# Spectrum pieces multiplied in place, turned products read back by halves, and a new written-out order in a convolution-plus-attention kernel

## The chip, the cores and the metric

The kernel runs on one core of one Trainium2 chip. A core has four engines that matter here, each with its own instruction stream worked off in order: PE (matrix multiply, whose weight loads are shown apart as PEld), DVE (vector), ACT (scalar and activation functions) and POOL. SP is a fifth stream, which in this kernel only issues DMAs. The engines wait for each other by semaphores. The metric is the device time of one execution in microseconds (us). The kernel before takes 303.53 us, the median of 9 runs between 301.97 and 305.27 us.

## What is computed

Two branches over the same input of 2048 rows by 512 channels are mixed by a gate:

```python
g = _sigmoid((x * gate_w).sum(-1, keepdims=True))
a = _A_ref(x, ...)            # long convolution of every channel
b = _B_ref(x, ...)            # linear attention with 32 heads of 16
return g * a + (1 - g) * b
```

Branch `a` builds a kernel of 2048 taps for each channel, `K = einsum("dn,dnl,dn->dl", Cc, exp(dt*A*l), dB).real`, pads it and the input to 4096, multiplies their Fourier spectra and transforms back; then it adds `u * Dskip`. Branch `b` forms `q, k, v`, applies for each head the feature map `concat(softmax(q @ w_phi), softmax(-q @ w_phi))` to `q` and `k`, sums `kv` and `z` over all rows, and divides the numerator by the denominator before the output projection `wo`.

## The kernel before

**Stages.** The work runs through these stages, which overlap. The *front* loads input (`UD`) and parameters, builds trigonometric tables (`TB`, `TI`, `TJ`), the factored tables `Ctab` and `Dtab` of the taps, and transforms the input (first step `psA` L577 to `XAu`, second step `psB` L225 to `XU`), writing the input's spectrum to memory (`XUd`). The *key stage* takes the 16 row tiles through `pk` (PE L695), two exponentials `Ek` (ACT), a reduction `Zk` (DVE L707), the values `vp` (PE L727) to `vb`, a scaling `vr` (DVE L736) and the sum `kvp` (PE L744). It ends when DVE reads `kvp` (`zj`, L820) and `Mw` is formed. The *query stage* takes four blocks of 512 rows: four `pq` (PE L879), exponentials `Eq` (ACT), sums `zs` (PE), a short chain `den` between ACT and DVE, a row of factors `apm` that goes through memory (`apd`) and comes back spread over partitions (`aexp`), a product of each `Eq` piece with it (DVE L943), and for each of four row tiles eight `bps` matmuls (L955) and four `diagD` ones (L958), evicted to `bS`.

**Taps and convolution** run beside these. There are eight groups `h` of 64 channels. For each half group DVE forms `A` (L991, with a sum L1006 for the last four groups) and `R` from the tables `E` and `cs` (L998, L1000, L1001); PE sums their products in `kps` (L212); the result is evicted as `KD`, transformed (`psA` L1041 to `XA`, `psB` L1082 to `XK`). The spectrum comes in pieces of 1024 columns: a piece `U` of the input's spectrum is loaded, and DVE multiplies it by `XK` into a tile `t` (L1104). PE turns this back by a first step (`psz` L1118, evicted to `Zr`), which SP writes to memory (`Zd`) and reads back with rows and times exchanged (`ZT`, L1137). The second step (`psy` L1171 and L1177) starts from the attention result `bS` of the same rows and channels, so that one DVE operation with the gate (`o`, L1201) gives the output, which SP stores (L1209). The last 64 channels skip the way through memory: their products `tN` are turned back on chip by 256 small matmuls (L1150, `Z`) and `psy` L1191.

**Three sets of 128 channels and two of 64** pass through `transform`; each of the first three gives two `o` tiles, the 64-channel sets give one each, eight in all.

**Buffers.** Four-kilobyte tiles per partition: `U` has 2 buffers and `t` 2. `Eq` is one tile for a whole query block, 2 buffers. `ZT` is one 8-kilobyte tile for a set, 2 buffers, in memory that is opened only after the query stage (`fpool`); every `psy` therefore comes after the last `bps`.

**What sets the order.** `Plan` collects the work as about a thousand nodes with dependences and named buffers. The string `ORDER` is the order in which all nodes are issued, and so the order of each engine's stream and of SP's DMAs. `SIDES` says for each of 129 evictions from the matmul accumulators (PSUM) whether ACT (L558) or DVE (L556) does it: 28 of them are on DVE. `RINGS` picks PSUM buffers. ACT changes its function table 12 times (L75), since exponentials and sines are in different tables.

Of the kernel before, what the change touches and what calls it, by code (L numbers as in the profile page):

```python
# [10 lines left out]
ACT = mybir.ActivationFunctionType  # L11
ALU = mybir.AluOpType
F32 = mybir.dt.float32
BF16 = mybir.dt.bfloat16
# [77 lines left out]
class Plan:  # L92
# [3 lines left out]
    ORDER = ("05020K0b0001080L0e0q0n0k0h0s0r0c0i0f0g04060t0l070d0m0o0O0N0Z0P0Q0R0-0S0p0M0T0_100U0V0W03091116171218130Y1419150X1a1b1c"  # L96
             "0u2x1p1d1i1e1j1f1k0a2D2E1w2F2G2H2I2J2L2M2N2O1l1S2K0j1q1t1u1r1v1s1L2P2R2S2Q2T2V1x2X1Q1z1y1A1B2U1E1O1C2W1R2Y2Z1D2_311F2-"
             "303334351M1G1N371H1I1P1K1T1V1g1h1J1m0y3639383a3b3c3d3e1U3f3g3h1W3i1X1Y2y3j3k3l3m3n3o3p3q0z3r3t1Z1-1_3s20213u223v232728"
             "3x3w3y292A2a242b252c3z3A2B0B0C2f2g320v0w0x2h2i2d3R3B2e2z0D2j2o2l2k2p2q3C3P3Q2n2s2r2m2t0A3S0E0F260G3D3E3G3F0H0I0J453J3M"
             "3N3H3I3K2u1n3L3O1o2v2w2C444b3-46473T639741424e4c4f3U4q4r8R8S3V4d8T4g4h4i4j4m8U4n4t4k4u8V8W4o4s4x4l4v4w4y4p4B4F4C4G4I4J"  # L100
             "4D8X8Y4z4A4E4U4V4H4K4L3_4M4X8Z3X40984Y914W924N4Q4O4R4S8-4_4P938_90949550534Z3Y999a969c9e4T9b9d9B9f4-9m575a5851549g5e52"
             "5955565b5c9C5f9h3W5d5m5n5p5i9o9i9D5q5g5h5o5r5j5k9j5t9E9k5s5x9n5u9p5y9l5l5B5C5E9F435v5F5z9G9q9r9t5D9u9s5G5w5I5A5Q5J5R5M"
             "5N5T5U5H9H9I5S5K9v9w5X5Y5O5_9J5V5L5P5W605Z619N5-62649O9K9P9x9y6566489z9AaPaRaSaW6768696b6a6d6c6e6f9T9UaQaUa29L9M9Q9V9R"
             "6g6i9W9X9Yada3a46ka5ae9S6hafa6496mag4aa7ao3Z6l6jah6naTaX6V6o9Z6XaV6W6p9-aY6Z6q9_6r6s6Y6taZb2b3b46ub5b96v6w6x6ybhbi6B6C"
             "a-a_6_b0b16D70bjb6a06-71b7b8babkblbb72bm6z6A6F7374bc6Ear756G6J6K7677a8as78a9bdbebfbgbn6Lboapai6Haqcvcwat6Ia16MajbCakbp"
             "bD6NcxcBbq6O6Pbtbubvcy6Q79cCaabz7a7bbAab7eac7fbrbKal7c7d7i6R7jam7kbscz7g7han7m7nbB7obLbM6Tbwau6ScEbxbEbyav6U7ycDbVaw7z"
             "bNbO7lbPbWaxbX7AaybF7CcAbG7B7E7p7qbYc47F7D7GcFc57sbZcMcN7Hb-7I7J7K7LbHbIbJcGdjc6cH7r7t7ubQc77v7wbR7M7NcScIcObScPcQc8c9"
             "7O7x8b8d7PcJ7Q7RbT8f7T8c8hcTcKcVcU7SducR7X8e8gcW8i8jcL8kcX8lb_8m7UbU7Vdkdl7Y7W8n7_7ZcYcZc08oc-c_d0ef7-8p8q8r80c1caegcb"
             "81828sc2dvc3dmdxdydnd18wd2dw8t8ucc83do8x8veld3d585d4d68AdpdI8y8B8CdqdJcd8z8EdFdrds8FdG8GdzdQ8DehdRdS8486dHdt878HemdKce"
             "dAdBdC88898ad7dT8I8KdDd8dUd9dE8J8LdddVen8M8Oewexde8Neyei8P8QejdadfdbdcdgekeHdhdLdMdWdXazeIeJaCdNcfaAcgdYaBaFaDeoepf1aE"  # L110
             "f2f3f4eqaGerescheteuf5evdZf7f8ezaKeKcleAaLeLf9faeBeMf6fbcmd-dOciaHdPd_eCeNeDaMaNficnfofccocpeOePeQeEeRe2fdaIeFaJfefgfh"
             "ffdie0flfmfjeGfkfne1aOe3e4cjfpfrfsckcqeSeTeUcreVcsctcufqe5ftfufvfwfxe6eaebe7e8eWeXeYe9fyecedeeeZe-fzfAfBfCe_f0")
    SIDES = ("0000010000011010100001110000010000001111110000000001000011001000000010000000000100011000000001000010000000000100010000"
             "00000010000")
    RINGS = ("1010110001110101000000000000000000100022222222222222222222222222222222000002222222222222222222222222222222200000000000"
             "0000000000000000000000000000000000000000000000000000000000000000003333333330030000003")
# [690 lines left out]
def queries_and_convolution(P, tc, nc, g, psum, sh, sp, sl, kv, bank, evict):  # L807
# [38 lines left out]
    mw = []  # L846
# [21 lines left out]
    for b in range(4):  # L868
        Q = Bag()
        eq = []  # L870
        for m in range(4):
            box = Bag()

            def pq(b=b, m=m, box=box, Q=Q):
                if m == 0:
                    Q.e = g.eqp.tile([128, 4, 2, 512], BF16, name="Eq", tag="r8")
                box.ps = bank("pq")
                for kt in range(4):
                    nc.tensor.matmul(box.ps[:], lhsT=g.Wqp[:, kt, 128 * m:128 * m + 128], rhs=g.xT[b][:, kt, :],  # L879
                                     start=(kt == 0), stop=(kt == 3))  # L880

            def qe(m=m, box=box, Q=Q):
                for sg in range(2):
                    act(out=Q.e[:, m, sg, :], in_=box.ps[:], func=ACT.Exp, scale=(1.0 if sg == 0 else -1.0))
                box.ps = None
            a = P.add("PE", 1.0, pq, [sh, sp, sk] + ([a] if m else []), take=["bk"] + ([] if m else ["r8"]))
            eq.append(P.add("ACT", 1.22, qe, [a], drop=["psum"], tab="L"))

        def zz(Q=Q):
            Q.z = g.psA.tile([128, 4, 128], F32, name="zs", tag="acc", bufs=1)  # L890
            for m in range(4):
                e = Q.e[:, m, :, :]
                for i in range(4):
                    nc.tensor.matmul(Q.z[32 * i:32 * i + 32, 0:2, :], lhsT=at.SZ[:, m, :], rhs=e[:, :, 128 * i:128 * i + 128],
                                     start=(m == 0), stop=(m == 3), tile_position=(0, 32 * i), skip_group_check=True)
                for sg in range(2):
                    for i in range(4):
                        nc.tensor.matmul(Q.z[32 * i:32 * i + 32, 2 + sg, :], lhsT=at.SS[:, sg, m, :], rhs=e[:, sg, 128 * i:128 * i + 128],
                                         start=False, stop=(m == 3), tile_position=(0, 32 * i), skip_group_check=True)
# [35 lines left out]
        for m in range(4):  # L935
# [6 lines left out]
            def de(m=m, box=box, Q=Q):  # L942
                nc.vector.tensor_tensor(out=Q.e[:, m], in0=Q.e[:, m], in1=box.x[:], op=ALU.mult)  # L943
                box.x = None
            x = P.dma(0.6, 1.8, ax, [zw], take=["ax"], move=2.2)
            em.append(P.add("DVE", 0.69, de, [x, eq[m]] + em[-1:], drop=["ax"]))
        for i in range(4):
# [3 lines left out]
            def pbm(b=b, i=i, box=box, Q=Q):  # L951
                box.ps = bank("bps")
                for k in range(8):
                    m, sg = k // 2, k % 2
                    nc.tensor.matmul(box.ps[:], lhsT=Q.e[:, m, sg, 128 * i:128 * i + 128], rhs=g.Mw[:, 4 * sg + m, :], start=(k == 0), stop=False,  # L955
# [13 lines left out]
            pb = P.add("PE", 2.1, pbm, em + [pb] + mw, take=["bk"] + (["x4"] if i == 0 else []), drop=(["r8", "x4"] if i == 3 else []))  # L969
# [85 lines left out]
    def transform(XA, ready, Q, off, nd, far, last):  # L1055
# [11 lines left out]
        for r0 in range(0, 32, ns):  # L1067
# [3 lines left out]
            def ld(r0=r0, box=box):  # L1071
                box.U = g.cpool.tile([128, 2, no, ns, 64], BF16, name="U", tag="U", bufs=2)
# [22 lines left out]
            def tt(r0=r0, box=box, end=end):  # L1095
                if far:
                    o = box.t = g.cpool.tile([128, 2, no, ns, 64], BF16, name="t", tag="t", bufs=2)
                    o = o[:]
# [10 lines left out]
            tn.append(P.add("DVE", 1.22, tt, [x, u] + tn[-1:] + ([] if far else [sq]), take=(["t"] if far else []), drop=["XK", "U"]))  # L1109
# [20 lines left out]
            z = P.add("PE", 1.03, fi, [tn[-1]] + ([z] if r0 else []), take=[psq, "Zr"], drop=["t"])  # L1130
# [3 lines left out]
        def fr(th):  # L1134
            if th == 0:
                F.Z = g.fpool.tile([128, 4096], BF16, name="ZT", tag="ZT", bufs=2)[:, 0:32 * nd].rearrange("p (t d) -> p t d", d=nd)
            nc.sync.dma_start(out=F.Z[64 * th:64 * th + 64], in_=F.Zd[:, 2 * th:2 * th + 2].rearrange("t x r d -> (x r) t d"))  # L1137
        for th in range(2 if far else 0):
            rn.append(P.dma(0.6, 1.8, lambda th=th: fr(th), wn + [sq] + [n.issue for n in rn[-1:]], take=(["Z"] if th == 0 else []), move=3.4 * nd / 128 + 0.3))
# [22 lines left out]
        for j0 in range(0, 16, nj):  # L1162
            box = Bag()
            end = j0 + nj == 16

            def py(j0=j0, box=box, end=end):
                if far:
# [5 lines left out]
                    for jj in range(nj):  # L1173
                        th = (j0 + jj) // 8
                        rows = slice(64 * th, 64 * th + 64)
                        for c in range(4):
                            nc.tensor.matmul(box.ps[32 * c:32 * c + 32, jj, :], lhsT=fc.TJ[rows, 4 * (j0 + jj) + c, :],  # L1177
                                             rhs=F.Z[rows, 4 * (j0 - 8 * th + jj) + c, :], start=False, stop=True, tile_position=(64 * th, 32 * c),
                                             skip_group_check=True)
                else:  # L1180
# [13 lines left out]
                if end:  # L1194
                    F.Z = None

            def ou(j0=j0, box=box):
                gb = g.gT[:, j0:j0 + nj]
                box.o = g.fpool.tile([128, nj, nd], BF16, name="o", tag="o", bufs=3)
# [7 lines left out]
            def st(j0=j0, box=box):  # L1207
                for c in range(4):
                    nc.sync.dma_start(out=ov[c, :, j0:j0 + nj, :], in_=box.o[32 * c:32 * c + 32])  # L1209
                box.o = None  # L1210
            y = P.add("PE", 1.15 if nj == 8 else 1.82, py, (rn[:1 + (j0 + nj - 1) // 8] if far else zn) + qdone[j0:j0 + nj] + ([y] if j0 else []), take=[psq, "o"],
                      drop=(["Z"] if end and far else []))
            o = P.add("DVE", 1.22, ou, [y], drop=["psum"])
            P.dma(1.95, 1.6, st, [o], drop=["o"], move=1.5)
# [22 lines left out]
def full_kernel(tc, A_u, A_A_re, A_A_im, A_B_re, A_B_im, A_C_re, A_C_im, A_log_dt, A_Dskip,  # L1237
# [7 lines left out]
    with ExitStack() as ctx:  # L1245
# [103 lines left out]
        def shift_keys():  # L1349
# [4 lines left out]
            g.eqp = pool(ca, "eqp", 2)  # L1354

        def shift_queries():
# [5 lines left out]
        P = Plan({"XAu": 1, "Ek": 2, "Zk": 2, "vr": 2, "vb": 2, "acc": 1, "r8": 2, "nrm": 1, "ax": 2, "x4": 5, "o": 3, "E": 4, "cs": 4, "A": 3, "R": 3, "KD": 1, "XA": 2,  # L1362
                  "XK": 2, "Z": 2, "Zr": 2, "U": 2, "t": 2}, {"ps": 2, "p0": 2, "bk": 3, "pf": 2})
# [63 lines left out]
```

## Time and profile before

| what | value |
|---|---|
| median of 9 runs | 303.53 us |
| the profiled execution | 302.38 us, span 300.5 us |
| DVE busy | 249.9 us (83%) |
| ACT busy | 236.2 us (79%) |
| PE busy | 218.6 us (73%) |
| 128x1024 eviction, DVE / ACT | 1.22 us / 1.02 us |
| 128x512 eviction, DVE / ACT | 0.68 us / 0.60 us |
| DVE first reads `kvp` (end of the key stage) | 130.57 us |
| last product L943 starts | 233.35 us |
| last `R` product starts | 268.64 us |

The span goes from the first to the last instruction of the profiled execution; the 1.9 us around it belong to its own time. "Idle before" is time in which an engine stood still just before an instruction, with the engine whose result ended it.

### The profile page before, as it was taken

How to read it: one execution, taken by the hardware profiler on the slowest of the kernel's cores; microseconds unless marked ns; L12 is line 12 of the kernel's file. 1: busy time of each engine (PE TensorE's matmuls, PEld its weight loads, DVE VectorE, ACT ScalarE, POOL GpSimd, SP SyncE). 2: the span in 40 equal slices, each digit the busy share in tenths (PEclk: the TensorE clock that was granted, in tenths of full speed). 3: DMA queues.
4: the chain of work that ended last, by engine and by line, in shares of the span. 5: the costliest groups of instructions: out<-in, count | busy, mean ns of one | idle time of the engine just before them, and what ended most of it. 6: DMA issues, size and time to landing. Idle time of an engine off the chain costs nothing.

```text
span 300.5 us, 10434 instructions
## 1 busy us (share of the span) xinstructions
PE 218.6 (73%) x4641; PEld 134.5 (45%) x4672; DVE 249.9 (83%) x401; ACT 236.2 (79%) x313; POOL 4.9 (2%) x17
## 2 busy tenths in 40 slices
PE   0056585347986999958988579999879978686960
PEld 0055464243432755542655434565544535454750
DVE  7849998899999899989878979989997958993431
ACT  2978998999999999798969799958888597446110
POOL 4000000000000000010000000000000000000000
PEclk9998959657998999986999999999999997779695
DMA  8996768969940000040231255553545746876933
GB/s 136 166 157 136 114 101 175 267 179 329 367 142 3 4 2 2 5 143 0 76 107 55 83 144 168 171 116 117 168 130 149 260 124 140 194 177 180 176 83 64
DMA packets 71357, 39.88 MB, mean 133 GB/s; under 512 B 57104, under 2 KB 63376, under 8 KB 71312
## 3 DMA queue, kind: packets, MB, share of 16 engines
q1 hardware_dynamic: 70256, 38.96, 52.7%
q8 instruction: 36, 0.59, 0.8%
q10 hardware_dynamic: 1056, 0.26, 0.6%
q14 instruction: 9, 0.07, 0.1%
HBM read 24.53 MB, written 14.94 MB: 131 GB/s over the span
## 4 chain that ended last, share of the span: by engine, by line
PE 39%; ACT 24%; DVE 15%; SPq 9%; issue 6%; DMA 4%; DVEq 0%; ACTq 0%
PE bps L955 9%; PE kps L212 6%; ACT E L83 5%; ACT cs L83 3%; PE pq L879 3%; ACT Ek L83 3%; SPq L1297 3%; DVE A L991 3%; ACT XU L558 2%; SPq L292 2%; PE psz L1118 2%; PE psB L1082 2%; PE vp L727 2%; PE psz L1150 2%; PE pk L695 2%
## 5 line engine op out<-in xcount | busy, mean ns | idle before, releaser
L991 DVE TENSOR_TENSOR A<-Ctab,Dtab 128x2048 bf16<-128x2048 bf16 x32 | 38.4, 1217 | 1.8 <-PE kps L212 1.8
L83 ACT ACTIVATE E<-args 128x1024 bf16<-128x1024 f32 x32 | 31.2, 1046 | 2.8 <-PE args L773 2.8
L83 ACT ACTIVATE cs<-args 128x1024 bf16<-128x1024 f32 x32 | 30.3, 1034 | 1.2 <-PE args L791 1.2
L955 PE MATMUL bps<-Mw,Eq 128*128 128x512 bf16 x121 | 29.0, 380 | 1.0 <-issue 1.0
L212 PE MATMUL kps<-R,A 128*32 128x64 bf16 x1536 | 26.8, 225 | 3.8 <-DVE R L1001 2.8
L577 PE MATMUL psA<-W,UD 128*64 128x256 bf16 x128 | 13.8, 380 | 20.7 <-DMA UD<-in_A_u_dram 18.7
L212 PEld LDWEIGHTS <-A 128*32 128x32 bf16 x1536 | 24.7, 152 | 8.6 <-issue 6.5
L998 DVE TENSOR_TENSOR R<-E,cs 128x1024 bf16<-128x1024 bf16 x32 | 21.9, 685 | 4.6 <-ACT cs L83 2.8
L1001 DVE TENSOR_TENSOR R<-E,cs 128x1024 bf16<-128x1024 bf16 x32 | 22.0, 688 | 0.6
L577 PEld LDWEIGHTS <-UD 128*64 128x64 bf16 x128 | 12.0, 206 | 22.0 <-DMA wc<-in_B_w_phi_dram 18.6
L707 DVE TENSOR_REDUCE Zk<-Ek 128x64 f32<-128x1024 bf16 x16 | 19.1, 1212 | 0.4 <-ACT Ek L83 0.4
L1104 DVE TENSOR_TENSOR t<-U,XK 128x1024 bf16<-128x1024 bf16 x28 | 18.0, 686 | 1.1 <-ACT XK L558 1.0
L83 ACT ACTIVATE Ek<-pk 128x512 bf16<-128x512 f32 x32 | 16.8, 606 | 1.8 <-PE pk L695 1.8
L955 PEld LDWEIGHTS <-Eq 128*128 128x128 bf16 x128 | 11.5, 98 | 15.1 <-issue 3.0
L83 ACT ACTIVATE Eq<-pq 128x512 bf16<-128x512 f32 x32 | 16.7, 627 | 1.7 <-PE pq L879 1.7
L695 PE MATMUL pk<-Wkp,xT 128*128 128x512 bf16 x59 | 16.5, 410 | 1.4 <-DVE vb L556 0.8
L225 PE MATMUL psB<-XAu,TB 64*128 64x128 bf16 x256 | 11.3, 245 | 8.2 <-ACT XAu L558 4.0
L727 PE MATMUL vp<-Wv,xT 128*128 128x512 bf16 x58 | 16.4, 394 | 0.6 <-issue 0.3
L1082 PE MATMUL psB<-XA,TB 64*128 64x64 bf16 (+1 forms) x640 | 12.2, 185 | 6.3 <-issue 1.6
L558 ACT CAST XA<-psA 128x1024 bf16<-128x1024 f32 x15 | 15.1, 1030 | 1.9 <-PE psA L1041 1.8
L1118 PE MATMUL psz<-t,TI 128*128 128x512 bf16 x50 | 15.6, 415 | 1.2 <-ACT XA L558 0.3
L558 ACT CAST Zr<-psz 128x1024 bf16<-128x1024 f32 x12 | 12.2, 1015 | 5.2 <-PE psz L1118 5.0
(179 smaller groups left out, 462.4 us busy)
## 6 DMA issues: line engine op xcount, KB each, us to landing
U<-XUd SPq DMA_DIRECT2D x16, 512.0 KB
XUd<-XUd SPq DMA_DIRECT2D x8, 512.0 KB
aexp<-apd SPq DMA_DIRECT2D x16, 256.0 KB
Zd<-Zr SPq DMA_DIRECT2D x14, 256.0 KB
XUd<-XU SPq DMA_DIRECT2D x8, 384.0 KB
ZT<-Zd SPq DMA_DIRECT2D x6, 512.0 KB
UD<-in_A_u_dram SPq DMA_DIRECT2D x4, 512.0 KB
out_dram<-o SPq DMA_DIRECT2D x32, 64.0 KB
```

Source lines behind the costliest of these rows:

```text
L83: i = self.nc.scalar.activation(**kw)
L212: nc.tensor.matmul(kps[32 * dj:32 * dj + 32, g4, e, :], lhsT=A[q][:, o, :, :, d].rearrange("p a b -> p (a b)"), rhs=R[ri][:, d, :], start= ...
L558: nc.scalar.copy(out=o, in_=i)
L577: nc.tensor.matmul(box.ps[64 * e:64 * e + 64, i, :], lhsT=g.UD[:].rearrange("p t (e g) -> p g e t", e=2)[:, gw * h + 4 * g4 + i, e, :], rh ...
L695: nc.tensor.matmul(box.ps[:], lhsT=g.xT[st // 4][:, kt, ss], rhs=g.Wkp[:, kt, :], start=(kt == 0), stop=(kt == 3))
L707: nc.vector.tensor_reduce(out=K.Z[:, u, :, :], in_=K.E[:, u, :, :].rearrange("p g (h f) -> p g h f", f=16), axis=mybir.AxisListType.X, op= ...
L727: nc.tensor.matmul(box.ps[:], lhsT=g.xT[st // 4][:, kt, ss], rhs=g.Wv[:, kt, :], start=(kt == 0), stop=(kt == 3))
L955: nc.tensor.matmul(box.ps[:], lhsT=Q.e[:, m, sg, 128 * i:128 * i + 128], rhs=g.Mw[:, 4 * sg + m, :], start=(k == 0), stop=False, skip_grou ...
L991: nc.vector.tensor_tensor(out=c.A[q][:].rearrange("p o a b d -> p (o a) b d"), in0=Ct.to_broadcast([128, 8, 8, 32]), in1=Dt.to_broadcast([ ...
L998: nc.vector.tensor_tensor(out=c.R[o][:, :, 32:64], in0=E[:, :, 32:64], in1=x, op=ALU.mult)
L1001: nc.vector.tensor_tensor(out=c.R[o][:, :, 0:32], in0=E[:, :, 0:32], in1=x[:, :, ::-1], op=ALU.mult)
L1118: nc.tensor.matmul(box.ps[:, hb], lhsT=fc.TI[:, k].rearrange("p t h a -> p (t h a)"), rhs=rhs, start=(k == 0), stop=(k == 1))
```

## The change

It has four parts. (1) The product of a spectrum piece is written over `U` itself; `t` goes, `U` has 3 buffers, and a buffer of `U` comes free after `psz` has read it instead of after the product. (2) `Eq` becomes four tiles for each block, 8 buffers of a quarter of the size; all four are given back together as before. (3) The turned products are read back by halves of the rows: each set of 128 channels fills two tiles of half the size, each by two DMAs, so 14 reads replace 8. The first half of the first two sets uses the tile `ZA`, in memory that exists during the query stage, so their `psy` needs only the first two query blocks, and its output is written over the tile's own first part. All others use `ZB`, 3 buffers, after the query stage. (4) New strings: another order for all engines and SP, another choice of evictions (37 of 129 on DVE, 28 before) and of PSUM buffers.

```diff
-    ORDER = ("05020K0b0001080L0e0q0n0k...
+    ORDER = ("050K080b090L0P0e020001040a...
...
-                    Q.e = g.eqp.tile([128, 4, 2, 512], BF16, name="Eq", tag="r8")
+                    Q.e = [None] * 4
+                Q.e[m] = g.eqp.tile([128, 2, 512], BF16, name="Eq", tag="r8")
...
-                box.U = g.cpool.tile([128, 2, no, ns, 64], BF16, name="U", tag="U", bufs=2)
+                box.U = g.cpool.tile([128, 2, no, ns, 64], BF16, name="U", tag="U", bufs=3)
...
-                    o = box.t = g.cpool.tile([128, 2, no, ns, 64], BF16, name="t", tag="t", bufs=2)
-                    o = o[:]
+                    box.t = box.U
+                    o = box.t[:]
...
-            z = P.add("PE", 1.03, fi, [tn[-1]] + ([z] if r0 else []), take=[psq, "Zr"], drop=["t"])
+            z = P.add("PE", 1.03, fi, [tn[-1]] + ([z] if r0 else []), take=[psq, "Zr"], drop=["U"])
...
-        def fr(th):
-            if th == 0:
-                F.Z = g.fpool.tile([128, 4096], BF16, name="ZT", tag="ZT", bufs=2)[:, 0:32 * nd].rearrange("p (t d) -> p t d", d=nd)
-            nc.sync.dma_start(out=F.Z[64 * th:64 * th + 64], in_=F.Zd[:, 2 * th:2 * th + 2].rearrange("t x r d -> (x r) t d"))
...
+        early = [nd == 128 and Q < 2 and hf == 0 for hf in range(2)]
+        zk = ["ZA" if e else "ZB" for e in early]
+        F.Z = [None, None]
+
+        def fr(hf, u):
+            if u == 0:
+                F.Z[hf] = (g.cpool if early[hf] else g.fpool).tile([128, 2048], BF16, name=zk[hf], tag=zk[hf], bufs=(1 if early[hf] else 3))[:].rearrange("p (t d) -> p t d", d=nd)
+            i = F.Zd[16 * u:16 * u + 16, 2 * hf:2 * hf + 2] if nd == 128 else F.Zd[:, 2 * u:2 * u + 2]
+            nc.sync.dma_start(out=F.Z[hf][64 * u:64 * u + 64], in_=i.rearrange("t x r d -> (x r) t d"))
...
+            ok = far and early[j0 // 8]
...
+                    if ok:
+                        box.o = F.Z[j0 // 8][:, 0:8]
```

What the new order moves, read from the two instruction streams: SP loads all four parts of `UD` ahead of the small parameters, and turns `wTq` ahead and `wTk` behind the writes of `pz`. DVE takes two `XAu` evictions ahead of its first parameter products, and the masks, `Wphi` and `diagD` move from the front's start to its middle. POOL makes `tgc` ahead of the small `one`. The first `A` product moves ahead of the selector `selE`, the second ahead of the first `Zk`. On ACT the eight `cs` of the second table set run before `KVT` and `Mw` instead of around them, and two `E` come ahead of the first `Eq`. The last table set's first `cs` come after the last `bps` tile of the third query block instead of after the second of the fourth. One `psy` with its `o` and its four stores goes into the query stage; the second `ZA` one stays in the end part.

## The prediction

> **What bounds the kernel now.** I read the page first, its busy times and its slices, then busy time by stretches of 20 us, then the sum of waits, and last the time line of DVE and of the end. No operation is removed, so the question is where engines stand idle.
>
> ```profile
> PE 218.6 (73%) x4641; PEld 134.5 (45%) x4672; DVE 249.9 (83%) x401; ACT 236.2 (79%) x313; POOL 4.9 (2%) x17
> DVE  7849998899999899989878979989997958993431
> ACT  2978998999999999798969799958888597446110
> ```
>
> ```profile
> 0.00:20.00 20.00, 1.33 (x13) 1.36 (x15) 13.03 (x50) 12.28 (x12) 3.56 (x15) 1.00 1.10 153
> ...
> 100.00:120.00 20.00, 18.68 (x494) 10.85 (x493) 19.78 (x26) 19.39 (x34) 0.00 (x0) 1.00 0.01 3
> ...
> 180.00:200.00 20.00, 19.57 (x262) 10.34 (x265) 19.21 (x27) 17.87 (x24) 0.00 (x0) 1.00 0.59 171
> ...
> 280.00:300.50 20.50, 10.06 (x494) 8.55 (x490) 5.01 (x5) 2.02 (x2) 0.00 (x0) 0.75 0.50 95
> ```
>
> In each stretch the numbers are PE, PEld, DVE and ACT busy. From 20 to 240 us DVE works 9 parts in 10 or more, ACT hardly less, and in the key stage (100 to 120 us) both are full. Around 180 to 240 us PE is full too. DVE's idle time up to 260 us, summed over the stretches, is 29.6 us, 7.0 of them before 20 us. The end is a chain of latencies: DVE works 5.0 us of the last 20.5.
>
> ```profile
> DVE R L998 <- ACT cs L83: 2.8, 1, 2.8
> DVE Eq L943 <- DMA aexp<-apd: 2.8, 4, 1.3
> DVE den L916 <- ACT den L83: 1.2, 2, 0.7
> DVE t L1104 <- ACT XK L558: 1.0, 3, 0.4
> DVE pb L499 <- ACT trg L83: 0.9, 1, 0.9
> DVE den L909 <- ACT den L83: 0.8, 1, 0.8
> DVE pb L490 <- ACT trg L83: 0.7, 1, 0.7
> DVE vr L736 <- ACT vr L83: 0.7, 2, 0.4
> DVE Zk L707 <- ACT Ek L83: 0.4, 1, 0.4
> ```
>
> These are DVE's waits for ACT and for `aexp` before its last `R` (total, times, longest). They are short and spread, and they are what a new order could save.
>
> **Nine evictions go from ACT to DVE.** By kind, five net are 128x1024 and four 128x512. DVE rows: 1.22 and 0.68 us; ACT rows: 1.02 and 0.60.
>
> ```profile
> L556 DVE CAST vb<-vp 128x512 bf16<-128x512 f32 x7 | 4.6, 683 | 0.2 <-PE vp L727 0.2
> L556 DVE CAST XK<-psB 128x1024 bf16<-128x1024 f32 x5 | 6.1, 1222 | 1.1 <-PE psB L1082 1.1
> L558 ACT CAST XA<-psA 128x1024 bf16<-128x1024 f32 x15 | 15.1, 1030 | 1.9 <-PE psA L1041 1.8
> ```
>
> DVE gains 5 x 1.22 + 4 x 0.68 = 8.8 us of busy time. On the time line neighbouring instructions overlap by about 0.08 us (two products of 1.22 take 2.35), so by starts it is 5 x 1.14 + 4 x 0.60 = 8.1 us. ACT loses 5 x 1.02 + 4 x 0.60 = 7.5.
>
> I added up DVE's work by starts in both instruction orders to three marks. To `zj`, the end of the key stage: 113.4 before, 120.1 after, +6.7. To the last L943: 201.8 and 212.8, +11.0. To the last `R`: 231.2 and 237.1, +5.9. Behind it 10.4 and 12.7, because one eviction of `Z` and one more `o` stand there.
>
> *To `zj`, +4.0 us.* Of +6.7 some fits into idle time. From 20 to 131 us the waits of more than 0.1 us that DVE's time line names sum to 5.2 us. ACT, lighter, can shorten those it causes; PE's and the DMAs' stay. I take half, 2.6: +4.0. Ends: +1.5 (all absorbed) and +6.7 (none). The front's changed loads: `UD` ends PE's first wait at 18.67 us; the small loads that stood ahead of three quarters of it cost SP 1.62 and 0.52 us, so PE may start up to 2.1 us earlier, or not at all where the transfers themselves set it. But DVE now has two `XAu` first and no `Wphi`; its wait for `wc` (3.9 us, to 18.90) becomes one for `psA`, at 18.67 + 1.14 less what `UD` gains, 17.7 to 19.8 us. That is -1.2 to +0.9; I take 0. Parameters queued behind `UD` delay ACT's `dtc` (17.34 before) and so DVE's L407, which now has 2.3 us of `XAu` ahead of it. `wTk` behind `pz` is needed by `Wkp` only, which moves to the end of the front; `pk` waits for it if it is late: 0, up to +2.0 (the row of one `wTq` issue, 1.97). POOL's `one` waits for `tgc` (2.0 us), before `w1`; PE needs that only at 18 us: 0.
>
> *From `zj` to the last L943, +4.4 us.* Before, 103 us hold 88.4 us of DVE work; after, 92.7. The additional work is not waste: more of the end's work is ahead of this mark. I leave the idle time of about 15 us as it is, since ACT has as much more to do there: two `E` ahead of the first `Eq`, and the last table load. PE has one `psy` pass (0.63 + 1.04), one `psz` (0.9) and one half `kps` (1.1) more ahead of the last `bps`. Bounds: half the 9.4 us of waits named there vanish (-0.3), or 5 us more arise at the joints of the stages (+9.4). One such joint is certain: all eight `cs`, 7.6 us, now stand ahead of `KVT`.
>
> *From the last L943 to the last `R`, -6.4 us.* Before, 35.3 us for 29.4 of work, with a wait of 2.8 for `cs` and 1.3 for `kps`. After, 24.3 of work. The first `cs` of the last set come earlier and that 2.8 us wait goes; but the third and fourth `cs` stand behind the second `bps` tile of the last block (2.5 us each on the time line), so DVE, after two sums and four `R`, waits for them some 1.5 us. Later ones stand behind `KD` and two `XA`. I take 4.6 us idle for 5.9. Ends: none of the gain in idle and 3 us more (-2.1), or 4.1 saved (-9.2).
>
> *The end, +0.7 us.*
>
> ```profile
> 269.39 1.10 PE L212 MATMUL kps<-R,A 128*32 128x64 bf16 x60 [0.80 <-DVE R L1001]
> 271.65 1.05 PE L1041 MATMUL psA<-W,KD 128*128 128x256 bf16 x8 [1.16 <-ACT KD L558]
> 280.29 3.59 PE L1150 MATMUL psz<-TI,tN 128*32 128x64 bf16 x133 [0.26 <-DVE tN L1104]
> 281.61 16.28 SPq L1209 DMA_DIRECT2D out_dram<-o  x20
> 292.59 1.23 DVE L1203 TENSOR_TENSOR o<-psy,gT 128x1024 bf16<-128x1024 f32 x1 [1.93 <-PE psy L1191]
> ```
>
> Here is the chain after the last `R`: `kps`, `KD`, `psA`, `XA`, `psB`, `XK`, `tN`, L1150, `psy`, `o`, stores. Only one `ZA` pass has left this part, while two passes that stood ahead of the last `R` now stand in it: six `o` become seven. One pass costs PE 1.67 us. It sits between `kps` and `psA`, where PE stood still 1.16 us: +0.5. All four `tN` now come without an `o` between them, -1.4; another `psy` splits L1150, +1.7; `Z` on DVE behind two `o`, about 0. Sum +0.8, and I take +0.7, as SP's last twelve stores may follow closely anyway. Ends -1 and +2.5.
>
> **What I cost at nothing.** The product in place is the same 28 instructions of 0.69 us. A `U` buffer comes free only after `psz`, so the next load, and on SP whatever stands behind it (`aexp`, `apd`), waits longer. SP waited 25.1 us in all for the product before; the cover is the third buffer, and most loads are issued a whole piece ahead. Without it, see the second rival; below nothing it can't go, as no wait of DVE was for `U`. The four `Eq` tiles come free together, so only the taking is finer: 0, at best the 1.7 us that ACT's `Eq` waited for `pq`. Six more reads cost SP about 6 x 0.62 us of issue (the median of L1137), in stretches where it waits anyway; at most 3.7.
>
> The Trainium skill, "DMA: Bandwidth & Descriptors", section "Anatomy of one DMA", gives a fixed cost of about 2.0 us for each DMA, nearly all of it the receipt; six more in series would by that be an estimated 12 us, which would turn the sum into +14.7. That page's figure is for DMAs issued from POOL, and no row here has such a wait in series.
>
> A second rule speaks against the change: "Perfetto Trace Analysis", section "Optimizing Scalar/DVE Operations", advises giving work to ScalarE when DVE is saturated, and here nine evictions go the other way. Taken strictly, all of DVE's +5.9 us would show and the sum would be +6.6. The rows show 29.6 us of idle DVE, so I don't take it strictly.
>
> **Sum.** +4.0 + 4.4 - 6.4 + 0.7 = +2.7 us on the profiled 302.38, that is 305.1. This execution lies 1.15 us under the median of 303.53; carried over, 306.2 us.
>
> **Rivals.** (A) *Faster: the lighter ACT ends DVE's waits for it.* The waits for ACT in the list above are 8.5 us without `aexp`. If all go, where I counted 3.9 of them as gone (2.6 and 1.3), the sum is +2.7 - 4.6 = -1.9, and with the 2.8 for `aexp` -4.7: 298.8 to 301.6. It decides from 4.2 us more than I counted. For it: ACT is 7.5 us lighter, and DVE's idle time is in many small pieces. Against: by 130 us ACT was itself full only because DVE fed it, and it is no earlier than DVE's `zj` lets it be. (B) *Much slower: SP holds the query blocks.* A `U` load waiting for `psz` keeps the next `aexp` behind it. DVE's longest wait for `aexp` was 1.3 us; once for each of four blocks, with the 2.5 us of a `bps` tile behind it at two of them, adds 5 to 10: 311 to 316. Against: only one `U` load stands between two `aexp` pairs. (C) *Nothing to measure:* PE, full from 180 to 240 us, sets the last `bps`, and DVE's additional work lies beside it; only the end's +0.7 and some 0.5 remain, 303 to 305. Half a per cent, 1.5 us, is about what can be told here.
>
> **Chances and range.** My own case 0.38, (A) 0.31, (B) 0.15, (C) 0.16. So faster 0.31, same 0.16, slower 0.53. The ends of the four terms sum to -9.0 and +16.5, which will not come together; taking in (A) and the near half of (B) the range is 298 to 312. My own case alone is 305.1 to 309.
>
> **What the profile after would show.** DVE busy near 258.8 us and ACT near 228.7; `zj` near 134.5 us instead of 130.57; the last L943 near 241.8; the last `R` starting near 270.5; then some 32 us to the end. If `zj` is at 132 or earlier, (A) is at work. If DVE waits more than 6 us for `aexp`, or SP's waits at the `U` loads hold the queue while `apm` is ready, (B). My forecast would be wrong above all if the joint at `KVT` or the `cs` behind `bps` cost another time than I took from their places in the order.

## The result, and the profile after

The changed kernel takes 306.16 us, the median of 16 runs between 303.67 and 308.81; beside it the kernel before took 302.86 us (51 runs). The ratio is 1.0098, with a 95% interval of 1.0074 to 1.0123: 1% slower, some 3 us. The profiled execution took 304.69 us (span 302.8), 2.3 us more than the profiled one of before. Medians are over all runs, ratios over the fast runs of both kernels, so the two can differ in the third digit. In the changed kernel line numbers behind `ORDER` are one higher up to the end of the key stage, two higher from the query stage on (the query product L943 is now L945), and 7 to 13 higher from the read-back on.

First the page of the changed kernel: busy times, then DVE, ACT and PE's granted clock in 40 slices.

```profile
PE 219.8 (73%) x4640; PEld 135.3 (45%) x4672; DVE 257.0 (85%) x410; ACT 228.9 (76%) x304; POOL 4.9 (2%) x17
...
DVE  7669999998999999997999879999968697995540
ACT  2879997958899999999969679967765885965000
...
PEclk9997765555899999995999759999987999979985
```

DVE gained 7.1 us and ACT lost 7.3, about what nine evictions weigh. The hole is in the three slices from 220 to 242 us (the 30th to the 32nd), where DVE is at 6, 8, 6 tenths and was at 9, 7, 9. The busy times by stretches (PE, PEld, DVE, ACT, POOL, granted clock, DMA share, GB/s) show it too: before, from 220 to 240 us, DVE was busy 17.18 us and PE 18.29, at a clock of 1.00.

```profile
0.00:20.00 20.00, 2.56 (x24) 2.59 (x26) 12.90 (x46) 11.92 (x11) 3.51 (x15) 1.00 1.12 153
100.00:120.00 20.00, 19.09 (x560) 11.53 (x566) 19.79 (x28) 19.91 (x31) 0.00 (x0) 1.00 0.01 3
180.00:200.00 20.00, 19.74 (x320) 10.62 (x322) 18.88 (x26) 19.09 (x26) 0.00 (x0) 0.99 0.60 159
220.00:240.00 20.00, 15.52 (x242) 8.24 (x241) 14.97 (x22) 12.97 (x15) 0.00 (x0) 0.83 0.52 140
280.00:302.80 22.80, 10.30 (x528) 8.13 (x528) 7.94 (x8) 1.01 (x1) 0.00 (x0) 0.78 0.51 96
```

Up to the end of the last `R`, DVE works 4.8 us more than before (243.9 instead of 239.1) and stands idle 2.5 us less (27.8 instead of 30.3); that is the 2.3 us. Many of its waits changed names: those for `aexp` (2.8 us) are gone, that for `cs` went from 2.8 us to 0.5, and others came. From the list of waits (total, times, longest):

```profile
DVE XA L557 <- PE psA L1043: 4.3, 2, 2.2
DVE XAu L557 <- PE psA L578: 3.2, 2, 2.5
DVE TJ L381 <- ACT tj L83: 2.3, 1, 2.3
DVE den L918 <- ACT den L83: 2.1, 4, 0.7
...
DVE ZA L1214 <- DMA U<-XUd: 1.7, 1, 1.7
```

The last one is named after a DMA, but DVE's time line shows what it is: the early `o` stands ahead of two query products and waits for its `psy`, which PE runs from 223.41 to 224.4 us.

```profile
222.36 0.42 DVE L919 TENSOR_TENSOR den<-zs,den 128x256 f32<-128x256 f32 x1
224.52 1.23 DVE L1214 TENSOR_TENSOR ZA<-psy,gT 128x1024 bf16<-128x1024 f32 x1 [1.73 <-DMA U<-XUd]
225.66 1.28 DVE L945 TENSOR_TENSOR Eq<-Eq,aexp 128x1024 bf16<-128x1024 bf16 x2
227.85 1.23 DVE L557 CAST XK<-psB 128x1024 bf16<-128x1024 f32 x1 [0.91 <-PE psB L1084]
```

The end looks as before, with one `o` more ahead of the last stores; from the end of the last `R` to the end of the span it is 31.2 us in both.

```profile
271.26 1.51 PE L213 MATMUL kps<-R,A 128*32 128x64 bf16 x64
...
273.89 1.05 PE L1043 MATMUL psA<-W,KD 128*128 128x256 bf16 x8 [0.20 <-ACT KD L559]
...
291.70 8.59 SPq L1222 DMA_DIRECT2D out_dram<-o  x12
...
293.65 1.22 DVE L1216 TENSOR_TENSOR o<-psy,gT 128x1024 bf16<-128x1024 f32 x1 [1.90 <-PE psy L1203]
```

The predicted marks stand against the measured ones so (us; the middle columns are differences to before):

| step of the sum | predicted | measured | mark in the changed kernel |
|---|---|---|---|
| start to `zj` | +4.0 | +3.8 | 134.35 |
| `zj` to the last L943 | +4.4 | +6.8 | 243.9 (the second of a pair from 243.32) |
| last L943 to last `R` | -6.4 | -8.3 | 270.94 |
| the end | +0.7 | 0.0 | span 302.8 |
| sum | +2.7 | +2.3 | |

By these marks the total holds, and so does the first term; the two in the middle miss by 2.4 and 1.9 us in opposite directions. Whether the marks mean what the prediction says was the question for the chip.

### The profile page after: what moved, and what is told of

Read it like the earlier page. It is cut to its first block, busy times and chain, and to the rows that moved or that the text cites. A ratio compares the mean times of both kernels' runs of the same rounds, so it can differ in the third digit from the quotient of the medians.

```text
span 302.8 us, 10446 instructions
## 1 busy us (share of the span) xinstructions
PE 219.8 (73%) x4640; PEld 135.3 (45%) x4672; DVE 257.0 (85%) x410; ACT 228.9 (76%) x304; POOL 4.9 (2%) x17
## 4 chain that ended last, share of the span: by engine, by line
DVE 35%; PE 24%; ACT 19%; DMA 10%; issue 5%; SPq 4%; DVEq 0%; ACTq 0%
PE bps L957 6%; DVE A L993 5%; DVE Zk L708 4%; ACT cs L83 4%; PE kps L213 4%; DVE R L1000 4%; DMA UD<-in_A_u_dram 3%; DVE R L1003 3%; DVE U L1106 3%; DMA XUd<-XUd 2%; DMA aexp<-apd 2%; DVE vr L737 2%; PE psz L1120 2%; SPq L1310 2%; PE psz L1158 2%
## 5 line engine op out<-in xcount | busy, mean ns | idle before, releaser
L957 PE MATMUL bps<-Mw,Eq 128*128 128x512 bf16 x120 | 30.1, 392 | 1.2 <-issue 1.1
L226 PE MATMUL psB<-XAu,TB 64*128 64x128 bf16 x256 | 14.1, 288 | 8.4 <-ACT XU L559 3.9
L1106 DVE TENSOR_TENSOR U<-U,XK 128x1024 bf16<-128x1024 bf16 x28 | 18.0, 685 | 1.4 <-ACT XK L559 1.4
L1120 PE MATMUL psz<-U,TI 128*128 128x512 bf16 x51 | 16.8, 431 | 3.1 <-DVE U L1106 1.8
L559 ACT CAST XK<-psB 128x1024 bf16<-128x1024 f32 x13 | 13.4, 1040 | 4.6 <-PE psB L1084 4.6
L226 PEld LDWEIGHTS <-TB 64*128 64x128 bf16 x256 | 12.3, 131 | 10.3 <-issue 7.1
L559 ACT CAST XA<-psA 128x1024 bf16<-128x1024 f32 x13 | 13.4, 1036 | 3.7 <-PE psA L1043 3.7
```

The costliest lines, as they stand in the source:

```text
L226: nc.tensor.matmul(ps[:, e, sl, :], lhsT=fc.TB[rows, r, 1 - ri:3 - ri, :].rearrange("p a b -> p (a b)"), rhs=XA[rows, r, ri, :], start=(ri ...
L559: nc.scalar.copy(out=o, in_=i)
L957: nc.tensor.matmul(box.ps[:], lhsT=Q.e[m][:, sg, 128 * i:128 * i + 128], rhs=g.Mw[:, 4 * sg + m, :], start=(k == 0), stop=False, skip_grou ...
L1106: nc.vector.tensor_tensor(out=o[:, k], in0=box.U[:, k], in1=box.XK[:].rearrange("p s (o d) -> p o s d", o=no), op=ALU.mult)
L1120: nc.tensor.matmul(box.ps[:, hb], lhsT=fc.TI[:, k].rearrange("p t h a -> p (t h a)"), rhs=rhs, start=(k == 0), stop=(k == 1))
```

## Experiments

All ratios are to the kernel before, run beside each kernel on the same chip. The marks compared below come from single profiled executions: in five kernels whose work up to `zj` is the same, `zj` lies between 129.1 and 131.0 us, so a mark tells differences of 2 us and more, not less. Diffs are shortened; where a line names a string or a stream in words, it stands for the recorded strings.

### Taking the structure apart from the order

**The product in place and four `Eq` tiles, in the old order** (`parts12`). The kernel before with the edits below; four `U` loads also stand a few places later on SP, behind the `psz` whose buffer they need.

```diff
-                box.U = g.cpool.tile([128, 2, no, ns, 64], BF16, name="U", tag="U", bufs=2)
+                box.U = g.cpool.tile([128, 2, no, ns, 64], BF16, name="U", tag="U", bufs=3)
...
-                    o = box.t = g.cpool.tile([128, 2, no, ns, 64], BF16, name="t", tag="t", bufs=2)
-                    o = o[:]
+                    box.t = box.U
+                    o = box.t[:]
...
+                Q.e[m] = g.eqp.tile([128, 2, 512], BF16, name="Eq", tag="r8")
```

> The kernel before with only the product written over `U` (three buffers, free after `psz`) and the four `Eq` tiles; order and evictions as before, except that four `U` loads stand a few places later on SP, behind the `psz` whose buffer they need. My theory, that these parts cost nothing: ratio to the kernel before 0.998 to 1.003, and DVE waits for `aexp` about as before (2.8 us). Rival (B), SP holds the query blocks: 1.015 to 1.04, with DVE waiting more than 6 us for `aexp`.

Measured: 308.41 us, ratio 1.0215 (1.0162 to 1.0267). What the prediction had costed at nothing costs twice as much as the whole change. SP's queue shows where. Here are its issues from 232 to 255 us in this kernel (start, length of the group with its waits):

```profile
232.12 0.38 SPq L1074 DMA_DIRECT2D U<-XUd  x1
234.75 0.32 SPq L1129 DMA_DIRECT2D Zd<-Zr  x1
235.17 15.77 SPq L1074 DMA_DIRECT2D U<-XUd  x2
251.00 4.04 SPq L1138 DMA_DIRECT2D ZT<-Zd  x2
```

and in the kernel before:

```profile
236.41 3.38 SPq L1073 DMA_DIRECT2D U<-XUd  x2
244.74 2.40 SPq L1137 DMA_DIRECT2D ZT<-Zd  x2
```

The second of the two `U` loads waits for a buffer, which now comes free only after `psz`; the reads of `ZT` stand behind it and issue 6.3 us later. The first `psy` on PE waits for them, and the first two `o` on DVE wait for theirs:

```profile
257.79 1.04 PE L1178 MATMUL psy<-ZT,TJ 64*32 64x128 bf16 x32 [5.80 <-DMA ZT<-Zd]
...
258.88 1.23 DVE L1202 TENSOR_TENSOR o<-psy,gT 128x1024 bf16<-128x1024 f32 x1 [2.80 <-PE psy L1178]
...
267.12 1.23 DVE L1202 TENSOR_TENSOR o<-psy,gT 128x1024 bf16<-128x1024 f32 x1 [2.95 <-PE psy L1178]
```

Before, these two waited 0 and 0.59 us. The last `R` stands behind them on DVE and ends at 274.9 us instead of 269.3. This is rival (B)'s mechanism with another victim: DVE's waits for `aexp` rose only from 2.8 to 5.4 us, and the block's products came 1.8 us later.

**The same with four `U` buffers** (`inplace4`). This takes away what the load waits for, and the four loads stand at their old places on SP again:

```diff
-                box.U = g.cpool.tile([128, 2, no, ns, 64], BF16, name="U", tag="U", bufs=3)
+                box.U = g.cpool.tile([128, 2, no, ns, 64], BF16, name="U", tag="U", bufs=4)
```

> As the run of the first two parts in the old order, but `U` has four buffers (the memory of the two `U` and two `t` before), so no `U` load moves on SP. Theory formed from that run: its 6 us come from one `U` load that waits 15 us on SP for `psz` at 235 us and keeps the `ZT` reads behind it; with four buffers the ratio to the kernel before is 0.997 to 1.004 and the first `ZT` read issues near 244.7 us again. Rival: the product over its own input, or the `Eq` tiles, cost the time themselves: 1.015 to 1.025.

Measured: 302.06 us, ratio 0.997 (0.9929 to 1.0011). The 6 us are gone: they were the missing buffer, with the later places of the loads that it forces, and neither the product over its own input nor the `Eq` tiles. Four `U` buffers are the memory of the two `U` and two `t` before. The change takes one of the four away and has the tile `ZA`, which is just as large; no run has both in the query stage.

**Besides, the reads by halves** (`halves`). The changed kernel's code for the reads, but with no half early and four `ZB`:

```diff
-        early = [nd == 128 and Q < 2 and hf == 0 for hf in range(2)]
+        early = [False, False]
```

> The run with four `U` buffers and, besides, the reads by halves of the rows (14 reads, `ZB` with 4 buffers, none of them early), each set's reads at the places of the old ones. My prediction, that six more reads cost nothing: 0.995 to 1.004. Rival: they cost SP's issue time in series, up to 3.7 us, or the receipt of each: 1.006 to 1.015.

Measured: 301.51 us, ratio 0.9965 (0.9932 to 0.9998). Six more reads cost nothing that can be told here; by the two intervals, a cost of some 1.5 us could hide. The Trainium skill, "DMA: Bandwidth & Descriptors", section "Anatomy of one DMA", has about 2.0 us of fixed cost for each DMA issued from POOL. The estimate of 12 us made from it does not show here: the reads, issued from SP, do not wait for each other in series (two of them issue within 1.34 us, from 254.57). With `inplace4`, from which it cannot be told apart, this is the fastest version in this study, 1.3% under the changed kernel; against the kernel before, its interval just excludes no gain.

### Taking the order apart at `zj`

**New up to `zj`, old behind** (`newkeys`). The two orders have nearly the same work ahead of `zj`, so they can be joined there:

```diff
 # kernel before
-    ORDER, SIDES, RINGS up to zj: as before
+    ORDER, SIDES, RINGS up to zj: as in the changed kernel
```

> The kernel before (old buffers, 8 reads, old order behind `zj`), but everything up to `zj` in the new order and on the new engines. My sum: `zj` at about 134.4 us and a ratio of 1.010 to 1.013. Rival, the later `zj` is work brought forward: 0.997 to 1.003.

Measured: 302.85 us, ratio 1.0027 (0.9992 to 1.0062). `zj` is at 134.25 us, 3.7 late as in the changed kernel, and the time is that of before. The delay melts behind `zj`: 2.2 us when PE ends the last `mps` matmul for `Mw`, 1.2 at the first query product, -0.2 at the last `R`. The last two are less than a mark can tell, but the ratio says the same. Some 2.2 us of it are work brought forward: the gate's `gz`, `gT` and `zrow` (1.0) and one `XA` (1.14), besides three `cs` on ACT (2.9).

**Old up to `zj`, new behind** (`oldkeys`). The changed kernel with the opposite edit:

```diff
 # changed kernel
-    ORDER, SIDES, RINGS up to zj: as in the changed kernel
+    ORDER, SIDES, RINGS up to zj: as before
```

> The changed kernel, but everything up to `zj` in the order and on the engines of the kernel before; from there on as changed. My sum (the key stage costs about 4 us, the rest gives some back): `zj` back at about 130.6 us and 3.5 to 4 us off the changed kernel, ratio to before about 0.996. Rival, suggested by the first L945, which the changed kernel starts at 167.2 us (before: 167.9): the later `zj` is only work brought forward, and the loss arises in the query stage; then the ratio stays at 1.006 to 1.012.

Measured: 308.28 us, ratio 1.0211 (1.0164 to 1.0259). `zj` is back at 130.60 us, and the kernel is 1.1% slower than the changed one: neither theory had that. DVE's list of waits names the place:

```profile
DVE XA L557 <- PE psA L1043: 9.4, 2, 6.2
```

The new order behind `zj` puts KVT and `Mw` behind all eight `cs`. Where three of them, and the gate, are not yet done by `zj`, PE ends the last `mps` matmul for `Mw` 16.1 us after `zj` instead of 9.2 in the changed kernel. The early `zj` is worth nothing to this order.

### Engines of the evictions

**The engines of before up to `zj`** (`oldsidesK`) and **behind it** (`oldsidesQ`), with the changed kernel's order untouched (one `XA` eviction keeps its new engine in both). For instance, of the string `SIDES`:

```diff
-    SIDES = ("0011000010010011010001011000010000100111111100000011000001...
+    SIDES = ("0000010000011010100001110000010000001111110000000001000001...
```

> The changed kernel, its order untouched, but the evictions up to `zj` on the engines of the kernel before: net three of 128x1024 and two of 128x512 go from DVE back to ACT, 4.6 us of DVE's work by starts. My theory: six tenths of it show, `zj` 2.5 to 3 us earlier and the time 2 to 3 us down, ratio to before about 1.000. Rival (DVE is not what sets `zj`, or ACT is as full): `zj` within 0.7 us of 134.4 and the ratio still 1.007 to 1.012.

> The changed kernel, its order untouched, but the evictions behind `zj` (from the last tile of `Mw` on) on the engines of the kernel before: ten go back to ACT and seven to DVE, net one of 128x1024 and two of 128x512, 2.3 us of DVE's work by starts. My theory of the prediction (DVE's added work shows): ratio 0.999 to 1.005. Rival, by the run with the key stage's engines: each eviction is where its order needs it, and it gets slower: 1.015 to 1.03.

Measured: 311.02 us, ratio 1.0272 (1.0211 to 1.0334), and 311.20 us, ratio 1.0278 (1.0224 to 1.0332). In both DVE has less to do (252.8 and 254.4 us busy instead of 257.0), and both lose 1.7 to 1.8% against the changed kernel; for the first, neither expectation had that. In the first, ACT takes two `XAu` ahead of the small `dtc`, and DVE stands longest there:

```profile
DVE pt L408 <- ACT dtc L83: 4.7, 1, 4.7
...
20.79 0.69 DVE L408 SCALAR_TENSOR_TENSOR pt<-Are,dtc 128x512 f32<-128x512 bf16 x1 [4.65 <-ACT dtc L83]
```

But this wait is not the loss. In the changed kernel DVE does the two `XAu` in that time, waits 2.46 us for the first, and starts the same `pt` at 20.87 us:

```profile
18.60 2.36 DVE L557 CAST XAu<-psA 128x1024 bf16<-128x1024 f32 x2 [2.46 <-PE psA L578]
...
20.87 0.68 DVE L408 SCALAR_TENSOR_TENSOR pt<-Are,dtc 128x512 f32<-128x512 bf16 x1
```

DVE's steps fall behind those of the changed kernel only after it, in many small waits: by 1.4 us at 32.3 us, 3.6 at 54.1, 4.5 at 102.6 and 5.8 at `zj` (140.16). Which of the 15 moved evictions starts this is not shown. In the second, one place tells most of it. A DVE eviction of `Mw` stands ahead of work that is ready:

```profile
145.00 1.23 DVE L557 CAST Mw<-mps 128x1024 bf16<-128x1024 f32 x1 [7.40 <-PE mps L854]
```

The `R` products behind it start at 146.15 us instead of 140.73, and the first query product and the last `R` come 6.3 us later. So an eviction can cost several times its 1.2 us by what it stands ahead of. The Trainium skill, "Perfetto Trace Analysis", section "Optimizing Scalar/DVE Operations", says that giving some work to ScalarE may make sense when DVE is saturated. In the changed kernel DVE is 85% and ACT 76% busy, and both ways of doing so cost time here: the share of busy time alone did not decide.

### The price of work on DVE

To price DVE's time by itself, four `A` products of the kernel before are done twice, once in the key stage (`dveK`), once between the first and the last query product (`dveQ`):

```diff
-                nc.vector.tensor_tensor(out=c.A[q][:].rearrange("p o a b d -> p (o a) b d"), in0=Ct.to_broadcast([128, 8, 8, 32]),
+                for _ in range(2 if q == 1 and h < 2 else 1):
+                    nc.vector.tensor_tensor(out=c.A[q][:].rearrange("p o a b d -> p (o a) b d"), in0=Ct.to_broadcast([128, 8, 8, 32]),
```

> The kernel before with four of the `A` products of the key stage done twice (same result), 4.6 us of DVE's work by starts ahead of `zj`, nothing else. Prediction's reading (six tenths of what DVE gets there shows, and stays): `zj` 2.7 us later and a ratio of 1.008 to 1.011. Rival (a late `zj` is recovered behind it): `zj` 2.5 to 4.6 us later and a ratio of 1.000 to 1.004.

> The kernel before with four `A` products between the first and the last query product done twice (the second `A` of both halves of the groups h = 4 and 5, same result), 4.6 us of DVE's work by starts, nothing else. If DVE sets this stage as it sets the key stage: last `R` 3.5 to 4.6 us later, ratio 1.011 to 1.015; the changed kernel's 2.0 us of added DVE work between its first product and its last `R` would then nearly all show. Rival (C) of the prediction, PE sets the last `bps` and DVE's idle time takes it in: last `R` 0 to 1.5 us later, ratio 1.000 to 1.005.

Measured: 306.09 us, ratio 1.013 (1.0085 to 1.0176), `zj` at 135.60; and 304.09 us, ratio 1.009 (1.0058 to 1.0122), last `R` 2.8 us later, though `zj` came 1.1 us earlier. A repeated product added a little more than the 1.14 us by which the expectations had it. The first of the four in `dveK`, and the same place before:

```profile
87.72 2.47 DVE L992 TENSOR_TENSOR A<-Ctab,Dtab 128x2048 bf16<-128x2048 bf16 x2
...
87.53 1.22 DVE L991 TENSOR_TENSOR A<-Ctab,Dtab 128x2048 bf16<-128x2048 bf16 x1
```

That is 1.25 us for each, 5.0 us for four. In the key stage all of it shows at `zj` (5.0 us), and 1.3% of 302.24, 3.9 us, at the end: 0.8 us for each us (0.5 to 1.1 by the interval). In the query stage it is 0.9% of 302.13, 2.7 us: 0.55 for each (0.35 to 0.75), between the two cases that were written down. The two intervals overlap, so that the key stage is dearer is likely, not shown.

### The early `psy`

**Moved back a little** (`latepsy`): its pass goes behind the first `bps` tile of the third block, and its `o` behind the two products it stood ahead of. SP's order stays.

```diff
 # PE
-psA, psy (early), psA, psB, args, bps
+psA, psA, psB, args, bps, psy (early)
 # DVE
-o (early), L945, L945, XK, U product
+L945, L945, XK, U product, o (early)
```

> The changed kernel with the early `psy` behind the first `bps` tile of the third query block and its `o` behind the two L945 products and the `U` product that it stood ahead of. Theory: the 1.7 us that DVE waits for this `psy`, and PE's pass ahead of `bps`, come off the last L945: 1 to 2.5 us less than the changed kernel, ratio to before 1.001 to 1.006. Rival: the chain `KD`, `psA`, `XA`, `psB`, `XK` sets this stretch: 1.008 to 1.012.

Measured: 308.76 us, ratio 1.0213 (1.017 to 1.0256), slower than the changed kernel by 1.1%, which neither expectation had. The two products do come directly behind `den`, but the four stores of this `o` still stand on SP ahead of the next `aexp`, and now wait themselves:

```profile
SPq L1222 <- DVE ZA L1214: 7.5, 1, 7.5
```

DVE then waits 3.0 us for `aexp`, and 3.3 for the `psy`. So the run says that a moved step takes its stores along, and leaves open what the early `psy` costs where it stands.

**Not early at all** (`noearly`, `noearly3`): the structure of `halves`, but the changed kernel's order and engines; what used `ZA` follows behind the query stage. The two differ in `U` alone:

```diff
-                box.U = g.cpool.tile([128, 2, no, ns, 64], BF16, name="U", tag="U", bufs=4)
+                box.U = g.cpool.tile([128, 2, no, ns, 64], BF16, name="U", tag="U", bufs=3)
```

> The changed kernel's order and engines, but four `U` buffers and no `ZA`: the reads, `psy`, `o` and stores that used it stand behind the query stage instead, all in `ZB` (4 buffers). Theory: with the old order this structure is 0.35% under the kernel before, so the rest is the price of the new order; without the early `psy` the last L945 comes 1.5 to 2 us earlier, one `o` more stands in the end, ratio to before 1.000 to 1.007. Rival: the new order lives on the early `psy`, and the end gets longer by the pass, its `o` and its stores: 1.012 to 1.020.

> The same with three `U` buffers, as in the changed kernel, nothing else. Theory: the new order already issues each `U` load behind the `psz` that frees its buffer, so the third and the fourth buffer differ by less than 0.3% here, unlike the 1.9% in the old order. Rival: the hold on SP costs here too, 1% to 2% over the run with four.

Measured: 308.23 us, ratio 1.0205 (1.0156 to 1.0253), and 307.50 us, ratio 1.0179 (1.0135 to 1.0223). In the new order the fourth buffer brings nothing that can be measured. And without the early `psy` the new order is some 1% slower than with it.

## Why the prediction was right, and where it was not

The time was right, 306.2 against 306.16 us, and so were the sign and, within half a us, three of the four marks (`zj`, the last `R`, the end); the last L943 came 2.1 us later than forecast. That the total came out to within half a us is partly luck: the two middle terms miss in opposite directions, and the reasons fared worse than the marks. A reading at the start is also too round: DVE works "9 parts in 10 or more" in seven of the eleven stretches from 20 to 240 us, and 16.93 to 17.44 us of 20 in the other four.

- **To `zj`, +4.0.** The mark was right (+3.8), its place in the sum was not. `newkeys` has the same late `zj` and ends within 0.3% of before. The step that failed is "of +6.7 some fits into idle time ... I take half": about 2.2 of the 6.7 us are work brought forward, and the remaining 4.5, though DVE's time in this stage is dear (0.8 by `dveK`), are paid for elsewhere. One payment is in the trace: from 18 us to `zj` DVE stands 5.1 us idle in `newkeys` (116.25 less 111.17 busy) and 7.9 before (112.57 less 104.69), and PE ends the input's transform at 56.7 us instead of 61.8. The front, which the prediction took as 0, gained: all six kernels with the new front and its engines stand idle 5.1 to 5.4 us there, the seven with the old one 6.7 to 8.6. The 1.7 us that are left are less than a mark can tell.
- **`zj` to the last L943, +4.4, and on to the last `R`, -6.4.** Measured +6.8 and -8.3: together -1.5 against -2.0. The mark between them falls where work of one order stands ahead of it and of the other behind. The first query product starts at 167.2 us, where it started at 167.9 before, so up to there nothing is lost; from it to the end of the last `R` the stage is longer. Here it is before, in `newkeys` and in the changed kernel (length, then busy PE, PEld, DVE, ACT, POOL, granted clock, DMA share, GB/s):

```profile
167.86:269.33 101.47, 87.09 (x1506) 49.15 (x1520) 89.88 (x128) 78.41 (x101) 0.00 (x0) 0.95 0.56 155
169.08:269.09 100.01, 87.56 (x1520) 48.70 (x1520) 89.80 (x128) 77.65 (x101) 0.00 (x0) 0.97 0.56 156
167.23:271.63 104.40, 88.39 (x1507) 48.67 (x1515) 91.80 (x131) 76.89 (x101) 0.00 (x0) 0.91 0.56 148
```

Some 2.0 us of DVE work came in, and idle time: 12.6 us of it, where before has 11.6 and `newkeys` 10.2, that is 1.0 to 2.4 us more, where the prediction left it as it was. By `dveQ`'s 0.55 the work alone would be 1.1 us. From 220 to 240 us DVE works 14.97 us, against 17.18 before and 17.65 in `newkeys`; of these 5.0 us of idle time the wait for the early `psy` is 1.73.

- **The end, +0.7.** 0.0 measured; the mechanism (one `o` more, no `o` between the four `tN`) is as told, and the term within its ends. One pass of `psy` took PE 1.0 us there (272.70 to 273.69), not the 1.67 that the sum has for it.
- **Costed at nothing.** Right for the `Eq` tiles and the product (`inplace4`), and for the reads (`halves`). Wrong for `U`: "the cover is the third buffer, and most loads are issued a whole piece ahead" failed, by 1.0215 less 0.997, about 7 us, in the old order. In the new order that cost is not there: `noearly` with four buffers is no faster than `noearly3` with three. In the changed kernel SP still waits for `psz` at the `U` loads, 21.4 us in eight waits, but 6.8 us at the longest where it was 12.1 in `parts12`; that what stands behind these loads has time to spare is likely and was not tested.
- **Rival (A)**, faster by the lighter ACT, did not come. But counting the nine evictions as a burden on DVE does no better: in the new order, both ways of giving some of them back to ACT lost 1.7 to 1.8%. **Rival (B)**: the hold on SP is real, in the old order, and it holds `ZT` rather than `aexp`. **Rival (C)**: half right, as by `dveQ` somewhat under half of what DVE gets in the query stage vanishes in its idle time.

What the change costs is then best read from structure to order. With the order of before, in-place products and halves are neutral, or faster by a third of a per cent (0.9965). With the new order and engines on that structure it is 1.0205; the early `psy`, for which a `U` buffer is given up, brings it back to 1.0098. As `noearly` takes a step out of an order that was made with it, part of these 2.4% may be the gap it leaves. The new order up to `zj` is neutral on the old structure. So the loss lies behind `zj`, and by the marks behind the first query product; which of the many moves there makes the idle time was not settled, the run aimed at the joint (`latepsy`) having been spoiled by its stores. One rival no run isolates: PE's granted clock. Its mean over an execution has a median of 0.864 in the changed kernel's 16 runs and 0.886 to 0.891 in the runs of the kernel before beside the experiments. In the stage above it is 0.91 against 0.95, and 0.89 to 0.93 in all kernels with the new order behind `zj`. A low mean alone does not make the loss, as `newkeys` has 0.871 in its 12 runs and loses at most 0.6%; but whether the clock in this stage is a cause of the idle time or follows from it stays open.

## What to carry to other kernels

When a buffer is held longer, look at the in-order queue that fills it: what waits is the load, and what loses is whatever stands behind it there (here reads for another stage, 6 us). A mark that comes later is a loss only if the same work stands ahead of it in both orders; joining the two orders at the mark tells which. In a written-out order, engine and place of a step belong together: all six runs that changed one part of the new kernel alone were slower than it, so the parts are better compared with whole stages exchanged, or priced in the old order. Where a wait is long, look when the engine reaches the same step in the other kernel: in `oldsidesK` the longest new wait cost nothing, the small ones behind it 5.8 us.

## What was not expected of the hardware

PE's granted clock differed between the two kernels in whole stretches, and PE's busy time does not tell where. From 40 to 60 us it was 0.51 in the changed kernel and 0.76 before, with PE busy 11.78 and 11.24 us; from 160 to 180 us 0.75 and 1.00, with 14.80 and 13.41. From 220 to 240 us, where PE had just waited 2.04 and 1.10 us, it was 0.83 against 1.00; taken by single microseconds it was 0.50 in each from 225 to 231 us and 1.00 in each from 232 to 240. This is the first `bps` tile behind those waits, then the second, in the changed kernel's time line:

```profile
228.98 2.92 PE L957 MATMUL bps<-Mw,Eq 128*128 128x512 bf16 x7 [0.33 <-issue]
...
235.52 1.67 PE L957 MATMUL bps<-Mw,Eq 128*128 128x512 bf16 x7 [0.16 <-issue]
```

2.92 us against 1.67 for the same seven matmuls: here a wait of PE was followed by a slower stretch, so it may be paid a second time. What exactly sets the clock back was not tested.
